# Windowed attention and a gated MLP: transposed probabilities spread into the band matrix by DMA, and the first entry's x split straight from PSUM

## The chip, the cores and the metric

One Trainium2 chip, one core. The metric is the device time of one launch in microseconds: the median of several runs for the kernel before, and the same for the changed one. Engines are called PE (TensorE), DVE (VectorE), ACT (ScalarE), POOL (GpSimd) and SP (SyncE, which issues the DMAs).

## What is computed

Attention over 8 batch entries, 8 heads, 576 positions of 64, with two masks, and then a gated MLP over all 4608 rows:

```python
scores = scale * q @ k.T                       # scale = 1/8
rel = pos[:, None] - pos[None, :]
mask_plain = (rel >= 0) & (rel < 32)                       # heads 0 to 3
mask_dil = (rel >= 0) & (rel < 128) & (rel % 4 == 0)       # heads 4 to 7
attn = softmax(where(mask, scores, -1e9)); attn_out = attn @ v
x = attn_out.transpose(0, 2, 1, 3).reshape(4608, 512)
h = x @ w_in                                   # 512 x 2048
g = h * sigmoid(1.702 * h)
out = g @ w_out                                # 2048 x 512
```

The weights come as float64.

## The kernel before

The host reorders the positions of the dilated heads by residue mod 4, so that each head has a band of 32 keys. The work has two kinds.

*Attention units.* A unit is one batch entry `b` and one pair of heads `c` (0 to 3), 32 in all, numbered i = 4b + c. `load_qk` and `load_v` fetch its inputs. `scores` makes blocks of 32 queries by 64 keys in PSUM (`sp`), `exponents` masks them (DVE, `pr` and the row minimum `mx`) and exponentiates (ACT, row sum `sm`); DVE normalises (`sm`, `pr`) and transposes the 32x32 blocks into `ct`. Then the transposed blocks are spread into `bt`, whose columns hold the probabilities as a band matrix with zeros elsewhere: eight copies per head or pair of heads, from one group of 32 partitions to another, on ACT or DVE. The two halves of `weigh` multiply `v` with `bt` on PE (24 matmuls, `av` in PSUM, "the product" below); ACT copies `av` to `xm` (512 of the entry's 576 positions) and to `xr` (the last 64, for a ninth group).

*MLP groups.* Eight groups of 512 positions (one per entry, `m0` to `m7`) and one of the 8 x 64 leftovers (`r`). `split_x` splits x into a float32r high part `xh` (ACT) and the remainder `xl` (DVE or POOL). For each of 16 slices f, `up` makes `hp` with 12 matmuls of 128x512 (4 blocks of x times 3: high by high, high by the weights' low part, low by high), ACT and DVE gate it, and `down` adds 12 more into four `acc` banks. A weight slice is decoded from float64 by `decode` (32 slices, n = 2f and 2f + 1): a load to a `cell`, three ACT passes and three or four DVE or POOL passes of 512 columns, giving `wih`, `wil`, `woh`, `wol`. All of this falls into the first group; entry 0's attention stands ahead of it, entry 1's beside it, and entry b + 1's attention runs beside group b from then on.

*Order.* Every step is an operation in `Plan` with a cost for each engine that may do it, an urgency, and keys that it reads and writes. `ordered` runs these through a list scheduler with those costs and emits each engine's instructions in that order; engines, and SP's queue of DMAs, work strictly in it. Waits come from the tile framework. DMAs count their completion on eight counters in turn, so each one waits for the one eight places earlier.

Units of entry 0 use `qk`, `v` and the buffer `second` in turn. There is one `pr`, `mx`, `sm`, `ct` and one `bt`.

Of the kernel before, what the change touches and what calls it, by code (L numbers as in the profile page):

```python
# [7 lines left out]
F32 = mybir.dt.float32  # L8
# [8 lines left out]
P = 128  # L17
# [14 lines left out]
class Plan:  # L32
# [27 lines left out]
    def ordered(self):  # L60
# [8 lines left out]
        port = [0.0]  # L69
# [11 lines left out]
        while any(open_):  # L81
# [10 lines left out]
            free[e] = when + (cost - 2.0 if e == DMA else cost)  # L92
# [12 lines left out]
def tile_windowed_attention_then_gated_mlp(  # L105
# [38 lines left out]
    xr = fixed([P, NC, B * LT], F32, "xr")  # L144
    pr = fixed([P, 2, QT, W], F32, "pr")
    mx = fixed([P, 2, QT], F32, "mx")
    sm = fixed([P, 2, QT], F32, "sm")
    ct = fixed([P, 2, QT, W], F32, "ct")
    bt = fixed([P, 2, QT, P + 32], F32, "bt")
# [19 lines left out]
    V.memset(sm, 1.0)  # L169
    V.memset(pr, 0.0)  # L170
    V.memset(bt, 0.0)
# [19 lines left out]
    def decode(n, urgency):  # L191
# [8 lines left out]
        else:  # L200
# [5 lines left out]
        taken = {8: ("qk1",), 9: ("qk1", "v1")}.get(n, ())  # L206
        low, top = (raw.bitcast(U32).rearrange("p (n t) -> p n t", t=2)[:, :, j] for j in range(2))
        value = word.bitcast(F32)

        add({DMA: 3.5}, urgency, lambda e: load(raw, src), (), (R, *taken))  # L210
# [8 lines left out]
            (R, R + "l"), (E,))  # L219
        add({ACT: 0.56}, urgency, lambda e: A.activation(hi, value, AF.Copy), (E,), (key,))  # L220
        add({DVE: -0.61, POOL: 1.35}, urgency, lambda e: pair(e, lo, value, f32(hi), ALU.subtract), (E,), (key,))

    def attention(b, c, urgency):
# [3 lines left out]
        z = i % 2 if b != 1 else 0  # L227

        spare = second.bitcast(F32).rearrange("p j n -> p (j n)")

        def load_qk(e):
            flat = spare[:, 0:2 * S] if z else temp([P, 2 * S], F32, "qk", f"qk_{i}")
            u["qk"] = flat.rearrange("p (a s) -> p a s", a=2)
            load(u["qk"], qk[i])

        def load_v(e):
            n = 2 * QT * D
            flat = spare[:, 2 * S:2 * S + n] if z else temp([P, n], F32, "v", f"v_{i}")
            u["v"] = flat.rearrange("p (a t d) -> p a t d", a=2, t=QT)
            load(u["v"], vp[i])  # L240


        late = [f"w{x}{f}" for x in "io" for f in range(NF - 3, NF)] if b >= FIRST else []
        add({DMA: 3.7}, urgency, load_qk, late if z else (), (f"qk{z}",))
        add({DMA: 3.0}, urgency, load_v, late if z else (), (f"v{z}",))

# [20 lines left out]
        def exponents(a, t):  # L267
            n = min(P, S - P * t)
            box, key = pr[0:n, a, t], f"{a}.{t}"
# [7 lines left out]
        def weights(hs):  # L277

            n, heads = hs.stop - hs.start, range(hs.start, hs.stop)
            boxes = [f"{a}.{t}" for a in heads for t in range(QT)]  # L280
# [7 lines left out]
            for a in heads:  # L288
                add({POOL: 0.69, DVE: -0.41}, urgency, lambda e, a=a: pair(
                    e, pr[:, a], pr[:, a], sm[:, a, :, None].broadcast_to([P, QT, W]), ALU.mult),  # L290
                    sums, [f"pr{a}.{t}" for t in range(QT)])
            turned = [f"ct{a}" for a in heads]
            for to in (0, 32):
                add({DVE: 0.07 + 0.165 * n}, urgency, lambda e, to=to: V.transpose(
                    out=ct[:, hs, :, to:to + 32], in_=pr[:, hs, :, 32 - to:64 - to]), probs, turned)
            for m in range(8):
                j, prev = m % 4, m // 4
                q = slice(32 * j, 32 * j + 32)
                if not prev:
                    dst, src = bt[q, hs, :, 32 * j:32 * j + 32], ct[q, hs, :, 0:32]  # L300
                elif j:
                    dst, src = bt[32 * j - 32:32 * j, hs, :, 32 * j:32 * j + 32], ct[q, hs, :, 32:64]
                else:
                    dst, src = bt[96:128, hs, 0:4, 128:160], ct[0:32, hs, 1:5, 32:64]
                add({ACT: 0.19 + 0.152 * n, DVE: -(0.19 + 0.07 * n)}, urgency,
                    lambda e, dst=dst, src=src: copy(e, dst, src), turned, [f"bt{a}{m}" for a in heads])

        for hs in (slice(0, 1), slice(1, 2)) if b < FIRST else (slice(0, 2),):
            weights(hs)

        def weigh(hf):
# [4 lines left out]
            def product(e):  # L316
                u["av", hf] = av = bank([P, 288], place, f"av_{i}_{hf}")
                for m, (t, lo, hi, col) in enumerate(parts):
                    for a in range(2):

                        T.matmul(av[D * a:D * a + D, col:col + hi - lo], u["v"][:, a, t], bt[:, a, t, lo:hi],  # L321
# [3 lines left out]
                (f"v{z}", *(f"bt{a}{m}" for a in range(2) for m in range(8))), (place, "product"))  # L325
            left = slice(LT * b, LT * b + LT)
            pieces = []
# [184 lines left out]
```

## Time and profile before

| | us |
|---|---|
| median of 3 runs | 925.05 (923.9 to 926.47) |
| profiled execution, its own time | 924.66 |
| its span, first to last instruction | 922.7 |
| PE busy | 892.7 (97%) |
| DVE, ACT, POOL busy | 494.7 (54%), 407.2 (44%), 30.1 (3%) |
| mean granted clock of PE | 0.985 |
| DMA, share of 16 engines | 18.5% in the one queue of SP |

The profile gives for each engine the time that its instructions cover. Matmuls are pipelined and overlap in the record, so a PE busy share near 100% is not yet PE at its peak rate; how many matmuls start in a stretch tells that. Idle time of an engine is listed with what released it.

### The profile page before, as it was taken

Reading aid. Unit: us, or ns where it says so; the run is one execution under the profiler, and the core shown is the slowest. Engines: PE = TensorE matmul, PEld = TensorE weight load, DVE = VectorE, ACT = ScalarE, POOL = GpSimd, SP = SyncE. Lnnn points to the kernel's source line nnn. Section 1 sums busy time; section 2 is a strip of 40 time slices with the busy share of each in tenths; the row PEclk is TensorE's granted clock in tenths of the full one; section 3 lists DMA queues with packets and bytes.
Section 4 is the critical chain, followed back from the end, with each engine's and each line's share of the span. In section 5 each row is a group of like instructions: output and inputs, shape, how many; then the busy total and the mean of one; then the engine's idle time right before and its main releaser. Section 6 shows DMA issues by size and latency. Waiting matters only on the chain.

```text
span 922.7 us, 17219 instructions
## 1 busy us (share of the span) xinstructions
PE 892.7 (97%) x6656; PEld 726.1 (79%) x6656; DVE 494.7 (54%) x1576; ACT 407.2 (44%) x1257; POOL 30.1 (3%) x32
## 2 busy tenths in 40 slices
PE   5699998999999999999999999999999999999997
PEld 4477786888888888888888888888888888888885
DVE  8899997655456337543654356534553433343332
ACT  7989878653366117621653156513641221121111
POOL 0011210000000000000000000000000000000000
PEclk9589999999999999999999999999999999999999
DMA  7365534211032003200221013100200010001002
GB/s 278 106 232 180 169 101 140 80 47 51 21 101 72 15 1 113 81 15 1 87 67 55 1 50 105 55 1 16 72 2 0 1 46 1 1 0 46 1 1 46
DMA packets 22674, 56.68 MB, mean 61 GB/s; under 512 B 6208, under 2 KB 6208, under 8 KB 22592
## 3 DMA queue, kind: packets, MB, share of 16 engines
q1 hardware_dynamic: 22592, 55.58, 18.5%
q8 instruction: 52, 0.85, 0.4%
q14 instruction: 30, 0.25, 0.1%
HBM read 46.14 MB, written 9.44 MB: 60 GB/s over the span
## 4 chain that ended last, share of the span: by engine, by line
PE 87%; ACT 5%; DVE 5%; DMA 1%; issue 1%; POOL 0%; DVEq 0%; SPq 0%; ACTq 0%
PE hp_m L369 36%; PE acc_m L406 12%; PE acc_m L407 12%; PE acc_m L410 12%; PE hp_r L369 5%; PE av L321 4%; PE sp L260 3%; PE acc_r L410 2%; PE acc_r L406 2%; PE acc_r L407 2%; ACT pr L273 1%; ACT bt L175 1%; DVE words L216 1%; DVE words L218 1%; DVE bt L177 1%
## 5 line engine op out<-in xcount | busy, mean ns | idle before, releaser
L376 ACT ACTIVATE g_m<-hp_m 128x512 f32<-128x512 f32 x128 | 76.1, 595 | 323.6 <-PE hp_m L369 323.3
L369 PE MATMUL hp_m<-xh,wih 128*128 128x512 f32 x512 | 206.4, 403 | 11.3 <-ACT xh L175 7.2
L379 DVE SCALAR_TENSOR_TENSOR g_m<-g_m,hp_m 128x512 f32<-128x512 f32 x128 | 87.8, 686 | 232.0 <-ACT g_m L376 230.9
L369 PE MATMUL hp_m<-xh,wil 128*128 128x512 f32 x512 | 201.8, 394 | 0.6 <-POOL wil L182 0.6
L369 PE MATMUL hp_m<-xl,wih 128*128 128x512 f32 x512 | 201.8, 394 | 0.0
L406 PE MATMUL acc_m<-gh_m,woh 128*128 128x512 f32 x512 | 201.2, 393 | 0.1
L407 PE MATMUL acc_m<-gh_m,wol 128*128 128x512 f32 x512 | 199.4, 389 | 0.0
L410 PE MATMUL acc_m<-gl_m,woh 128*128 128x512 f32 x512 | 142.3, 391 | 0.0
L369 PEld LDWEIGHTS hp_m<-xh,wih 128*128 128x128 f32 x512 | 97.0, 190 | 36.0 <-ACT xh L175 8.1
L273 ACT ACTIVATE pr<-pr,mx 128x64 f32<-128x64 f32 (+1 forms) x320 | 106.8, 336 | 32.5 <-DVE mx L270 32.4
L369 PEld LDWEIGHTS hp_m<-xl,wih 128*128 128x128 f32 x512 | 97.2, 190 | 22.1 <-DVE xl L182 1.6
L369 PEld LDWEIGHTS hp_m<-xh,wil 128*128 128x128 f32 x512 | 97.2, 190 | 20.1 <-POOL wil L182 1.1
L406 PEld LDWEIGHTS acc_m<-gh_m,woh 128*128 128x128 f32 x512 | 96.1, 188 | 21.1 <-ACT gh_m L175 0.3
L410 PEld LDWEIGHTS acc_m<-gl_m,woh 128*128 128x128 f32 x512 | 95.9, 188 | 20.5 <-POOL gl_m L182 0.2
L407 PEld LDWEIGHTS acc_m<-gh_m,wol 128*128 128x128 f32 x512 | 96.1, 188 | 19.6
L182 DVE TENSOR_TENSOR gl_m<-g_m,gh_m 128x512 fp32r<-128x512 f32 x126 | 90.0, 714 | 15.9 <-ACT gh_m L175 7.2
L270 DVE CUSTOM_DVE_ANT_0 pr<-sp,mask 128x64 f32<-128x64 f32 (+1 forms) x320 | 49.4, 213 | 49.0 <-PE sp L260 48.8
L175 ACT ACTIVATE bt<-ct 32x320 f32<-32x320 f32 (+3 forms) x171 | 70.3, 411 | 3.1
L273 ACT ACTIVATION_READ_ACCUMULATOR pr<-pr,mx 128x1 f32 (+1 forms) x320 | 60.3, 188 | 0.0
L177 DVE CAST gh_m<-g_m 128x512 fp32r<-128x512 f32 x107 | 45.5, 425 | 8.0
L175 ACT ACTIVATE xm<-av 128x224 f32<-128x224 f32 (+1 forms) x64 | 32.0, 505 | 30.6 <-PE av L321 30.6
L177 DVE COPY bt<-ct 32x320 f32<-32x320 f32 (+3 forms) x149 | 44.0, 295 | 2.6
(75 smaller groups left out, 782.6 us busy)
## 6 DMA issues: line engine op xcount, KB each, us to landing
qk<-qk_dram SPq DMA_DIRECT2D x18, 576.0 KB, 4.6
out_dram<-ost_m SPq DMA_DIRECT2D x32, 256.0 KB, 2.1
second<-qk_dram SPq DMA_DIRECT2D x14, 576.0 KB, 4.2
v<-vp_dram SPq DMA_DIRECT2D x18, 320.0 KB, 3.0
cell<-wi_dram SPq DMA_DIRECT2D x11, 512.0 KB, 3.7
cell<-wo_dram SPq DMA_DIRECT2D x11, 512.0 KB, 3.9
second<-vp_dram SPq DMA_DIRECT2D x14, 320.0 KB, 3.1
second<-wi_dram SPq DMA_DIRECT2D x5, 512.0 KB, 4.7
```

What stands on the lines that cost most here:

```text
L175: A.activation(dst, src, AF.Copy, scale=scale)
L177: V.tensor_copy(out=dst, in_=src)
L182: (V if e == DVE else G).tensor_tensor(out=dst, in0=a, in1=b, op=op)
L270: add({DVE: 0.15}, urgency, lambda e: V.tensor_tensor_reduce(out=box, in0=u["sp", a][0:n, t], in1=mask[0:n, t if dil or t == 0 else QT - 1 ...
L273: add({ACT: 0.33}, urgency, lambda e: A.activation(box, box, AF.Exp, bias=mx[0:n, a, t:t + 1], scale=-1.0, accum_out=sm[0:n, a, t:t + 1]), ...
L321: T.matmul(av[D * a:D * a + D, col:col + hi - lo], u["v"][:, a, t], bt[:, a, t, lo:hi], start=m == 0, stop=m == 2, skip_group_check=True)
L369: T.matmul(hps[f], st[:, f, c], mv[:, c], start=c == 0 and k == 0, stop=c == NC - 1 and k == 2)
L376: A.activation(self.g32, hps[f], AF.Tanh, scale=0.851)
L379: V.scalar_tensor_tensor(out=self.g32, in0=self.g32, scalar=1.0, in1=hps[f], op0=ALU.add, op1=ALU.mult)
L406: T.matmul(self.acc[j], woh[:, f, cols], gh, start=f == 0, stop=False)
L407: T.matmul(self.acc[j], wol[:, f, cols], gh, start=False, stop=False)
L410: T.matmul(self.acc[j], woh[:, f, P * j:P * j + P], self.g[f][1], start=False, stop=f == NF - 1)
```

## The change

Three things, and a new order that follows from them.

1. The eight copies from `ct` to `bt` become eight DMAs on SP's queue for a whole unit (`spread`), each 32 partitions by 320 elements (one has two pieces of 128). `ct` gets the two transposed halves as separate contiguous pieces and `bt` is laid out by column group, so that a partition's data is one run. `pr`, `mx`, `sm`, `ct` exist twice (by i mod 2). Entry 0 also has two `bt`; the second lies in the part of `wol` that the last four slices fill later, and POOL clears it.
2. For entry 0, `xh` and `xl` are made from `av` in PSUM directly, without `xm` and without `split_x`.
3. All inputs of entry 0 are loaded at once, units 2 and 3 into `xm` and `xr`, which are not otherwise used yet; weight slices 1 and 2 are ordered after the first spread.

The scheduler's model of a DMA changes: the queue is held 0.43 us, and the transfer takes 2.0 us and its size over a shared bus.

The diff, its core:

```diff
-            free[e] = when + (cost - 2.0 if e == DMA else cost)
+            free[e] = when + (0.43 if e == DMA else cost)
+            if e == DMA:
+                bus[0] = max(bus[0], when + 2.0) + cost / 360.0
+                cost = bus[0] - when
...
-    ct = fixed([P, 2, QT, W], F32, "ct")
-    bt = fixed([P, 2, QT, P + 32], F32, "bt")
+    cts = [fixed([P, 2, 2, QT, 32], F32, f"ct{j}") for j in range(2)]
+    late_bt = wol[:, NF - 4:].bitcast(F32).rearrange("p f n -> p (f n)")[:, 0:10 * QT * 32]
+    bts = [fixed([P, 5, 2, QT, 32], F32, "bt"), late_bt.rearrange("p (j a t n) -> p j a t n", j=5, a=2, t=QT)]
...
+    G.memset(late_bt, 0.0)
...
+    spare = [second.bitcast(F32).rearrange("p j n -> p (j n)"), xm.rearrange("p c n -> p (c n)"),
+             xr[:, 1:].rearrange("p b c n -> p (b c n)")]
...
-        z = i % 2 if b != 1 else 0
+        z = i if b == 0 else 0 if b == 1 else i % 2
+        y = i % 2 if b == 0 else 0
+        pr, mx, sm, ct, bt = prs[i % 2], mxs[i % 2], sms[i % 2], cts[i % 2], bts[y]
...
-            for to in (0, 32):
-                add({DVE: 0.07 + 0.165 * n}, urgency, lambda e, to=to: V.transpose(
-                    out=ct[:, hs, :, to:to + 32], in_=pr[:, hs, :, 32 - to:64 - to]), probs, turned)
+            for half in (0, 1):
+                add({DVE: 0.07 + 0.165 * n}, urgency, lambda e, half=half: V.transpose(
+                    out=ct[:, half, hs], in_=pr[:, hs, :, 32 - 32 * half:64 - 32 * half]),
+                    probs, [f"ct{i % 2}{half}{a}" for a in heads])
+
+        def spread():
             for m in range(8):
                 j, prev = m % 4, m // 4
                 q = slice(32 * j, 32 * j + 32)
                 if not prev:
-                    dst, src = bt[q, hs, :, 32 * j:32 * j + 32], ct[q, hs, :, 0:32]
+                    dst, src = bt[q, j], ct[q, 0]
                 elif j:
-                    dst, src = bt[32 * j - 32:32 * j, hs, :, 32 * j:32 * j + 32], ct[q, hs, :, 32:64]
+                    dst, src = bt[32 * j - 32:32 * j, j], ct[q, 1]
                 else:
-                    dst, src = bt[96:128, hs, 0:4, 128:160], ct[0:32, hs, 1:5, 32:64]
-                add({ACT: 0.19 + 0.152 * n, DVE: -(0.19 + 0.07 * n)}, urgency,
-                    lambda e, dst=dst, src=src: copy(e, dst, src), turned, [f"bt{a}{m}" for a in heads])
+                    dst, src = bt[96:128, 4, :, 0:4], ct[0:32, 1, :, 1:5]
+                add({DMA: 82}, urgency, lambda e, dst=dst, src=src: load(dst, src),
+                    [f"ct{i % 2}{prev}{a}" for a in (0, 1)], (f"bt{y}{m}", f"spread{i}.{m}"))
...
-                        T.matmul(av[D * a:D * a + D, col:col + hi - lo], u["v"][:, a, t], bt[:, a, t, lo:hi],
+                        T.matmul(av[D * a:D * a + D, col:col + hi - lo], u["v"][:, a, t],
+                                 bt[:, lo // 32:hi // 32, a, t],
...
+            if b == 0:
+                n = x_cols.stop - x_cols.start if not dil else 2 * P
+                add({ACT: 0.07 + n * 0.00083}, urgency, lambda e: copy(e, x_place(xh), x_of(u["av", hf])),
+                    (place,), (f"xh{c}.{hf}",))
+                add({DVE: 0.07 + n / 960}, urgency, lambda e: pair(
+                    e, x_place(xl), x_of(u["av", hf]), f32(x_place(xh)), ALU.subtract),
+                    (place, f"xh{c}.{hf}"), (f"xl{c}.{hf}",))
...
-    for n in range(2):
-        decode(n, 9.0 + n)
     for c in range(NC):
-        attention(0, c, 6.0 * c)
+        attention(0, c, c)
+        if c in (1, 2):
+            decode(c - 1, c + 0.5)
```

PE's order at the start, from the third unit's scores on. Before (L260 scores, L321 the product, L369 `up`; `64x160 x4` are four matmuls with 64 output rows and 160 columns):

```order
L260 MATMUL sp_0_246<-qk_194 32x32 x2
L260 MATMUL sp_0_246<-qk_194 32x64 x17
L260 MATMUL sp_1_279<-qk_194 32x32 x2
L260 MATMUL sp_1_279<-qk_194 32x64 x17
L321 MATMUL av_1_313<-bt,v_112 64x128 x2
L321 MATMUL av_1_313<-bt,v_112 64x160 x2
L321 MATMUL av_1_313<-bt,v_112 64x64 x2
L321 MATMUL av_0_331<-bt,v_112 64x160 x4
L321 MATMUL av_0_331<-bt,v_112 64x32 x2
L260 MATMUL sp_0_347<-second 32x32 x2
L260 MATMUL sp_0_347<-second 32x64 x17
L260 MATMUL sp_1_385<-second 32x32 x2
```

And now (L275 scores, L340 the product):

```order
L275 MATMUL sp_0_322<-xr 32x32 x2
L275 MATMUL sp_0_322<-xr 32x64 x17
L275 MATMUL sp_1_356<-xr 32x32 x2
L275 MATMUL sp_1_356<-xr 32x64 x17
L340 MATMUL av_1_390<-bt,v_119 64x128 x2
L340 MATMUL av_1_390<-bt,v_119 64x160 x2
L340 MATMUL av_1_390<-bt,v_119 64x64 x2
L340 MATMUL av_0_412<-bt,v_119 64x160 x4
L340 MATMUL av_0_412<-bt,v_119 64x32 x2
L340 MATMUL av_1_435<-wol,second 64x128 x2
L340 MATMUL av_1_435<-wol,second 64x160 x2
L340 MATMUL av_1_435<-wol,second 64x64 x2
```

The scores of all four units now stand ahead of the first product, and the first two products follow each other. By the fourth product 18 matmuls of `up` stood ahead before, and 12 now.

SP's order at the start, before, from its fifth DMA (L210 weight slices, L234 and L240 inputs):

```order
L210 DMA cell_104<-wi_dram 128x512
L210 DMA cell_105<-wo_dram 128x512
L234 DMA qk_194<-qk_dram 128x1152
L210 DMA cell_106<-wi_dram 128x512
L234 DMA second<-qk_dram 128x1152
L234 DMA qk_322<-qk_dram 128x1152
L210 DMA cell_104<-wo_dram 128x512
L240 DMA v_371<-vp_dram 128x640
```

And now, from its ninth DMA, with the waits (L323 is the spread; DMAHW0 to DMAHW7 are the eight completion counters):

```order
L254 DMA xr<-vp_dram 128x640 [waits DMAHW0_49]
L220 DMA second<-wi_dram 128x512 [waits DMAHW2_49,DMAHW1_49,PE_49]
L323 DMA bt<-ct_80 32x320 [waits DVE_49]
L323 DMA bt<-ct_80 32x320 [waits DMAHW3_49]
L323 DMA bt<-ct_80 32x320 [waits DMAHW4_49]
L323 DMA bt<-ct_80 32x320 [waits DMAHW5_49]
L323 DMA bt<-ct_80 32x2x128 [waits DMAHW6_49,DVE_49]
L323 DMA bt<-ct_80 32x320 [waits DMAHW7_49]
L323 DMA bt<-ct_80 32x320 [waits DMAHW0_49]
L323 DMA bt<-ct_80 32x320 [waits DMAHW1_49]
```

Ten loads stand ahead of the first spread; its eighth DMA shares a counter with the tenth load. The second unit's spread follows, and then three weight slices.

PE's order in the steady part, before, at the product of unit 9 (entry 2, c = 1):

```order
L369 MATMUL hp_m_4_2058<-xh,wih 128x512
L369 MATMUL hp_m_4_2058<-xh,wil 128x512
L369 MATMUL hp_m_4_2058<-xl,wih 128x512
L321 MATMUL av_1_2067<-bt,second 64x128 x2
L321 MATMUL av_1_2067<-bt,second 64x160 x2
L321 MATMUL av_1_2067<-bt,second 64x64 x2
L321 MATMUL av_0_2074<-bt,second 64x160 x4
L321 MATMUL av_0_2074<-bt,second 64x32 x2
L260 MATMUL sp_0_2083<-qk_1819 32x32 x2
```

And now:

```order
L407 MATMUL hp_m_5_2033<-xh,wih 128x512
L407 MATMUL hp_m_5_2033<-xh,wil 128x512
L407 MATMUL hp_m_5_2033<-xl,wih 128x512
L340 MATMUL av_1_2037<-bt,second 64x128 x2
L340 MATMUL av_1_2037<-bt,second 64x160 x2
L340 MATMUL av_1_2037<-bt,second 64x64 x2
L340 MATMUL av_0_2044<-bt,second 64x160 x4
L340 MATMUL av_0_2044<-bt,second 64x32 x2
L407 MATMUL hp_m_5_2033<-xh,wih 128x512
```

The product has moved from the middle of `hp` 4 to that of `hp` 5: between a unit's scores and its product stand 42 to 45 matmuls of 128x512 before and 52 to 62 now.

97 lines of the change are left out of this document (54 added, 43 removed).

## The prediction

> **What bounds the kernel now.** I read the stretches first (busy time of each engine per window, granted clock, DMA share).
>
> ```profile
> 20.00:30.00 10.00, 6.05 (x29) 4.26 (x30) 9.61 (x44) 9.80 (x41) 0.82 (x1) 0.53 0.68 226
> 30.00:40.00 10.00, 6.91 (x34) 4.52 (x33) 8.26 (x46) 9.78 (x37) 1.28 (x1) 0.62 0.21 71
> ...
> 100.00:150.00 50.00, 47.81 (x306) 37.34 (x305) 48.83 (x139) 43.35 (x119) 8.27 (x8) 1.00 0.37 118
> ...
> 200.00:300.00 100.00, 99.88 (x882) 81.66 (x881) 56.01 (x204) 49.14 (x169) 1.28 (x1) 1.00 0.18 58
> ```
>
> The columns are PE, PEld, DVE, ACT, POOL, clock, DMA share, GB/s. There are three regimes. From 200 us PE is full: 99.88 of 100 us. From 20 to 40 us ACT and DVE are full (ACT 9.80 of 10 us) and PE is not, at a clock of 0.53 to 0.62. From 53 to about 165 us, where the weights are still being decoded, DVE is nearly full (48.83 of 50) and PE loses a little. Then PE's own waits and its timeline, for the places:
>
> ```profile
> PE hp_m L369 <- ACT xh L175: 7.2, 3, 2.6
> PE sp L260 <- DMA qk<-qk_dram: 4.7, 1, 4.7
> PE hp_m L369 <- DVE g_m L379: 3.1, 2, 1.5
> ```
>
> ```profile
> 14.72 2.69 PE L321 MATMUL av<-bt,v 128*64 128x128 f32 x24
> ...
> 34.77 2.67 PE L321 MATMUL av<-bt,v 128*64 128x128 f32 x24
> ...
> 43.16 2.63 PE L321 MATMUL av<-bt,second 128*64 128x128 f32 x22 [0.72 <-DVE bt L177]
> 46.12 0.80 PE L369 MATMUL hp_m<-xh,wih 128*128 128x512 f32 x1 [0.33 <-ACT wih L220]
> ...
> 51.55 0.39 PE L369 MATMUL hp_m<-xh,wih 128*128 128x512 f32 x1
> ...
> 53.12 0.76 PE L260 MATMUL sp<-qk 64*32 64x32 f32 x38
> ```
>
> The named waits are short; what is lost at the start is mostly PE idling or at half clock behind a chain of ACT and DVE work: the fourth value product of batch entry 0 runs only at 43.16, and the 36 matmuls of the first three `hp` tiles are over at 53.12. Matmuls of 0.80 us become 0.39 at about 51.5, five microseconds after steady work began at 46.12. In the full regime the rate is
>
> ```profile
> 826.65 2.72 PE hp_r L369 x12
> ...
> 165.45 1.46 PE L321 MATMUL av<-bt,v 128*64 128x128 f32 x24
> ```
>
> 0.227 us each (2.72/12). The first row is from the chain that ended last, the second from PE's timeline: the first product of entry 2, the 430th matmul's place in program order, after which nothing is lost. So only the first 165 us can be won; behind them stands the same PE work whichever kernel runs, unless new waits appear there.
>
> **The change, part by part.** (1) The copies `bt<-ct` go from ACT and DVE. Busy time of the instructions that touch `bt` (PE, PEld, DVE, ACT):
>
> ```profile
> 0.00:60.00 60.00, 12.01 (x96) 10.49 (x96) 9.94 (x36) 9.52 (x29) 0.77 0.58 196
> 60.00:200.00 140.00, 11.48 (x168) 9.95 (x168) 12.43 (x39) 17.84 (x49) 1.00 0.41 135
> 200.00:922.70 722.70, 30.63 (x504) 28.45 (x504) 23.02 (x75) 42.91 (x93) 1.00 0.11 36
> ```
>
> That is 9.5 us of ACT and 9.9 of DVE (one memset, which stays, among it) before 60 us, and 17.8 and 12.4 between 60 and 200. After 200 us the 66 us lie under a full PE and are worth nothing.
>
> (2) In their place 8 DMAs for each of 32 units go on SP's queue, 256 in all. What one costs, the trace of before bounds only by other transfers: the spacing of issues, and time from issue to landing.
>
> ```profile
> 1.19 0.42 SPq L240 DMA_DIRECT2D v<-vp_dram  x1
> 1.65 0.43 SPq L234 DMA_DIRECT2D second<-qk_dram  x1
> ```
>
> ```profile
> out_dram<-ost_m SPq DMA_DIRECT2D x28, 256.0 KB, 2.1
> qk<-qk_dram SPq DMA_DIRECT2D x9, 576.0 KB, 4.6
> ...
> v<-vp_dram SPq DMA_DIRECT2D x9, 320.0 KB, 2.9
> ```
>
> Issues stand 0.46 us apart. A 40 KB spread between on-chip buffers lies nearest to the 256 KB store (2.1 us), below it if anything; 4.6 us (qk) is the far end, and zero the near one. I take 2.1: eight cost 7 x 0.46 + 2.1 = 5.3 us from `ct` to a usable `bt`, of which ACT and DVE pay nothing. A page of the Trainium skill speaks against the change: "SBUF — State Buffer", The DMA setup-cost knee, has each DMA pay a fixed 2 us or so and advises 128 partitions and one large transfer. By its figures (an estimate: 2 us + 41 KB at 218 GB/s for 32 partitions) one spread lands after 2.2 us, and the sum would not move by more than 0.1 us a unit.
>
> (3) At the start the queue matters. Six loads were issued by 3.7 us, and landed so (issue to landing):
>
> ```profile
> qk<-qk_dram SPq DMA_DIRECT2D x1, 576.0 KB, 4.0
> second<-qk_dram SPq DMA_DIRECT2D x1, 576.0 KB, 6.3
> cell<-wo_dram SPq DMA_DIRECT2D x1, 512.0 KB, 8.1
> ...
> second<-qk_dram SPq DMA_DIRECT2D x1, 576.0 KB, 5.9
> 9.95 0.33 SPq L234 DMA_DIRECT2D second<-qk_dram  x1
> ```
>
> A load waits for the bytes ahead of it: the ninth, issued at 9.95, landed at 15.85, with 4.6 MB through. In the changed kernel ten loads (4.7 MB) precede the first spread, so the tenth lands at about 16.1. And the rows of SP's order show that each DMA waits for the one eight places earlier; the eighth spread of unit 0 therefore waits for the tenth load.
>
> ```profile
> 9.59 1.25 DVE L177 COPY bt<-ct 32x160 f32<-32x160 f32 x5
> ...
> 12.25 0.34 DVE L294 STREAM_TRANSPOSE ct<-pr 128x160 f32<-128x160 f32 x1
> 6.34 0.35 ACT L273 ACTIVATE pr<-pr,mx 128x64 f32<-128x64 f32 x1 [4.32 <-DVE mx L270]
> ...
> 6.68 0.33 ACT L273 ACTIVATE pr<-pr,mx 128x64 f32<-128x64 f32 x1
> L175 ACT ACTIVATE xh<-xm 128x512 fp32r<-128x512 f32 x4 | 2.5, 620 | 0.0
> cell<-wi_dram SPq DMA_DIRECT2D x11, 512.0 KB, 3.7
> ```
>
> Unit 0's `ct` was complete at 12.6 with five copies (1.25 us) ahead of it on DVE, so now at 11.4. But its last spread is issued at 16.1 and lands at 18.2: the first product moves from 14.72 to 18.3, 3.6 us later. Then ACT, no longer interrupted by copies, runs the 40 exponentials 0.34 us apart from 6.34 on, with decode passes of 512 columns (0.62 us, as the `xh` row) between. Unit 1: `ct` at about 15.7, SP free at 16.6, spread landed at 22.3. Unit 2: exponentials over at 6.3 + 30 x 0.34 + 4 x 0.62 = 19.0, with half a microsecond of waiting 19.5; sums, product and transposes on DVE and POOL, `ct` near 22.2; three weight loads were issued at 20.2 to 21.2 and its last spreads wait for them (3.7 us for the first and more behind it, about 26.5): product at 28.7, where before it ran at 34.77. Unit 3: ten more exponentials, three decode passes and four of x, 19.5 + 3.4 + 3 x 0.62 + 4 x 0.6 = 27.1, `ct` near 28.8 by DVE's 1.7 us behind them, eight issues, landing at 34.5: product from 34.6 to 37.3, where before it ended at 45.8. The split of x from PSUM drops one ACT pass of 512 columns per c (the `xh` row, 0.62) and makes two subtractions where there was one on DVE; worth 0.5 us for the last c, inside the rounding. Of the 36 matmuls, 24 then stand behind the fourth product (18 before): 6 at half clock until about 40 us (five microseconds after steady work), 18 at 0.227: done at 44.0. **Gain to this point 53.1 - 44.0 = 9.1 us.** Bounds: 14 (no queueing, clock up at once) and 2 (the spread landing at 4.6 us in all four units, 10 us, less what the next unit's exponentials cover).
>
> (4) The decode stretch. From 53.12 to 165.45 PE does 393 matmuls (89.1 us) and
>
> ```profile
> 53.12:165.45 112.33, 6.74 (x380) 5.47 (x380) 1.00 0.47 155
> ...
> 53.12:165.45 112.33, 7.10 (x96) 5.90 (x97) 1.00 0.47 155
> ```
>
> 6.7 us of scores and 7.1 of products (first column after the length), 102.9 of 112.3: 9.4 us are lost, to gates that come late (the 3.1 above) and many small ones, with DVE nearly full. DVE and ACT lose about 12 and 18 us of work there. I take 4 us back. Bounds: 9.4 (all), and 3 us worse: weight loads now queue on SP behind spreads that wait for DVE's transposes, and a late decode is a late `hp`.
>
> (5) The steady part. The order puts the product of a unit 52 to 62 matmuls behind its scores (42 to 45 before).
>
> ```profile
> 275.62 1.00 PE L260 MATMUL sp<-second 64*32 64x32 f32 x76
> 286.98 1.46 PE L321 MATMUL av<-bt,second 128*64 128x128 f32 x24
> 282.28 0.90 DVE L294 STREAM_TRANSPOSE ct<-pr 128x320 f32<-128x320 f32 x2
> 283.63 2.39 ACT L175 ACTIVATE bt<-ct 32x320 f32<-32x320 f32 x5
> ```
>
> `ct` was ready at 283.2, the copies at 286.0, the product started at 286.98: 0.96 us of slack. With 54 matmuls for 45 it starts 2.0 us later, 5.8 us behind `ct`; 5.3 are needed. Cost nothing, by half a microsecond a unit. The cover is those matmuls; if it is gone, PE stands still for the difference in each of 24 units.
>
> The other parts cost nothing at the place where they stand: a POOL memset of 1600 columns runs while DVE waits for the first scores; smaller `pr` memsets lie before the first load lands; a second `pr`, `ct`, `bt` takes memory only. Later scores of units 2 and 3 need no buffer of unit 0 any more, which is in the walk.
>
> Sum on the profiled execution: 924.66 (span 922.7 and 1.96 around it) - 9.1 - 4.0 = 911.6; the median of the runs stands 0.4 higher, so 912.0.
>
> **Rivals.** *Steady stalls* (slower). If a spread lands later than about 2.6 us after issue, PE, which takes its work in order, waits in each of 24 units. At 2.9 us, the `v` row, 0.3 x 24 = 7 us come back; at 4.6, 2.0 x 24 = 48 us (947). It decides at 3.2 us, where 0.55 x 24 = 13 eats the gain. For it: the spread lies behind the next qk load in the same queue. Against it: that load is issued right behind the scores, 7 us earlier, and the nearest row, the store, has 2.1. Chance 0.10; time about 935.
> *The start gains little* (920 to 926): the queue holds the spreads back in every unit and the weight loads behind them in turn, so the gain of (3) is 2 and (4) is nothing or a loss. For it: 3.6 us are already lost on unit 0. Against it: from 20 us on the stretches show the DMA at a share of 0.21 to 0.68. Chance 0.12; about 922.
> *The decode stretch recovers fully* and the start is at its better bound: 924.7 - 11 - 9 = 905 or below; chance 0.06.
> *Spreads one after another.* If the fixed cost were paid eight times in series, a unit would need 8 x 2.1 = 17 us, 11 more than the order leaves: 24 x 11 = 264 us. The landings above (4.7, 8.0 and 11.3 us for the first, third and sixth of six loads, with 0.6, 1.5 and 2.9 MB through) go by bytes and overlap, so 0.01. The same page of the Trainium skill, in the rule that a DMA-bound transfer should be one DMA and not several, would make the kernel slower in this way; the trace does not agree for loads in flight together.
>
> **How the numbers follow.** My forecast, 905 to 920 about 912: 0.70. With the other cases and 0.01 for what I don't see, faster by over 0.3% (2.8 us; about what a measurement of this kernel can tell) gets 0.70 + 0.06 + 0.07 of the second rival, within 0.3% gets 0.05 of it, slower 0.10 + 0.01 + 0.01. The range reaches from the better bound, 902, to the second rival's worse end, 925; outside are the steady stalls.
>
> **What would show it.** First product near 18 us, fourth near 35, the first `acc` matmuls near 44; spreads landing near 2 us; DVE under 90% busy between 50 and 150; PE still 99.8% from 200 us on with no wait of `av` on a DMA. Wrong if a spread takes over 2.6 us, if `av <- DMA bt` stands among PE's waits in the steady part, or if decodes (`wih`, `woh`) become the wait of `hp` behind late weight loads.

## The result and the profile after

The changed kernel takes 935.08 us (median of 4 runs, 933.65 to 937.55), the kernel before 925.76 in the same rounds: a ratio of 1.0106, 95% interval 1.0078 to 1.0134. It is 9 us slower; 13 us faster had been forecast, and the range ended at 925. The profiled execution of the changed kernel is its longest, 937.55 us with a span of 935.8, so differences between the two traces (13.1 us of span) come out some 4 us larger than between the medians.

The stretches that the prediction read, now of the changed kernel (length, then PE, PEld, DVE, ACT, POOL busy, clock, DMA share, GB/s):

```profile
20.00:30.00 10.00, 6.53 (x50) 5.39 (x46) 6.99 (x42) 7.23 (x34) 0.72 (x1) 1.00 0.61 207
30.00:40.00 10.00, 6.35 (x33) 4.47 (x33) 8.36 (x18) 6.02 (x13) 0.00 (x0) 0.53 0.53 166
100.00:150.00 50.00, 49.06 (x332) 38.87 (x331) 39.36 (x89) 32.45 (x70) 7.22 (x6) 1.00 0.40 129
200.00:300.00 100.00, 98.90 (x870) 79.52 (x869) 44.96 (x164) 36.67 (x139) 2.25 (x2) 1.00 0.23 73
```

ACT and DVE did get their time back: ACT 7.23 of 10 us for 9.80 at the start, DVE 39.36 of 50 for 48.83 in the decode stretch. But PE is no fuller at the start, and from 200 us on it is 98.90 instead of 99.88. PE's waits name a new releaser (us in total, times, longest):

```profile
PE av L340 <- DMA bt<-ct: 10.5, 8, 2.9
PE sp L275 <- DMA qk<-qk_dram: 4.8, 2, 4.6
```

The products and the first `acc` matmul at the start, on PE's timeline (start, us, ...):

```profile
19.28 2.67 PE L340 MATMUL av<-bt,v 128*64 128x128 f32 x24 [2.90 <-DMA bt<-ct]
...
24.10 2.67 PE L340 MATMUL av<-wol,second 128*64 128x128 f32 x24 [2.16 <-DVE sm L302]
...
32.35 2.67 PE L340 MATMUL av<-bt,xm 128*64 128x128 f32 x24 [1.91 <-DMA bt<-ct]
...
39.98 1.87 PE L340 MATMUL av<-wol,xr 128*64 128x128 f32 x24
...
50.14 0.50 PE L445 MATMUL acc_m<-gh_m,woh 128*128 128x512 f32 x1
```

To see where the time goes I counted the 3456 matmuls of 128x512 (9 groups x 16 slices x 24) along PE's timeline and noted when the 37th, 769th and 3456th start. Their order among the attention work shifts a little between kernels, so the stretch from 769th to 3456th, 2688 matmuls with the steady attention beside them, is the clean one: in the runs below that keep the order of before it takes 660.5, 669.2 or 673.8 us, to within 0.1, and nothing between.

| start of matmul | 37th | 769th | 3456th | 769th to 3456th |
|---|---|---|---|---|
| before | 54.0 | 255.6 | 916.0 | 660.5 |
| changed | 50.1 | 253.5 | 929.9 | 676.3 |

So 3.9 us are won by the 37th matmul, 2.1 are left at the 769th, and 15.8 are lost in the part where the prediction had put zero. The first two columns scatter between executions: in before and three runs below with its order and its matmul length (256 and 5120 bytes, all tiles by 128) the 37th starts at 53.2 to 54.0 us and the 769th at 255.6 to 258.1, so 2 us at the 769th are within what single traces differ by. The last column is 660.5 in all four.

The loss of 15.8 us has two causes, as the experiments show. One is late spreads. The other is in no step of the prediction: even in the last group `r`, with no attention, no spread and no wait beside it, the matmuls are longer. Rows of PE by form, before (busy, mean ns):

```profile
L406 PE MATMUL acc_r<-gh_r,woh 128*128 128x512 f32 x64 | 24.9, 389 | 0.0
L407 PE MATMUL acc_r<-gh_r,wol 128*128 128x512 f32 x64 | 24.9, 389 | 0.0
...
L410 PE MATMUL acc_r<-gl_r,woh 128*128 128x512 f32 x64 | 17.6, 389 | 0.0
```

and changed:

```profile
L445 PE MATMUL acc_r<-gh_r,woh 128*128 128x512 f32 x64 | 25.4, 397 | 0.0
L446 PE MATMUL acc_r<-gh_r,wol 128*128 128x512 f32 x64 | 25.0, 391 | 0.0
...
L449 PE MATMUL acc_r<-gl_r,woh 128*128 128x512 f32 x64 | 18.0, 395 | 0.0
```

The three kinds of `hp_r` have 390 ns, for 389 before.

These instructions are the same in both kernels. Only the addresses differ: the second `pr`, `mx`, `sm` and `ct` take 2560 + 64 + 64 + 2560 bytes a partition, and everything allocated after `bt` (mask, second, words, g, ost, qk, v, gh, gl) has moved by these 5248 bytes; the weights and x have not.

### The profile page after: what moved, and what is told of

It is laid out like the page before. It is cut to its first block, busy times and chain, and to the rows that moved or that the text cites. A ratio compares the mean times of both kernels' runs of the same rounds, so it can differ in the third digit from the quotient of the medians.

```text
span 935.8 us, 17232 instructions
## 1 busy us (share of the span) xinstructions
PE 901.7 (96%) x6656; PEld 725.4 (78%) x6656; DVE 452.8 (48%) x1425; ACT 338.9 (36%) x1087; POOL 34.6 (4%) x36
## 4 chain that ended last, share of the span: by engine, by line
PE 82%; DVE 5%; ACT 4%; DMA 4%; SPq 2%; issue 1%; DVEq 0%; ACTq 0%
PE hp_m L407 33%; PE acc_m L445 11%; PE acc_m L449 11%; PE acc_m L446 11%; PE hp_r L407 5%; PE av L340 4%; PE sp L275 2%; SPq L323 2%; ACT pr L288 2%; PE acc_r L445 2%; PE acc_r L449 2%; PE acc_r L446 2%; DMA bt<-ct 1%; DMA second<-wi_dram 1%; DMA cell<-wo_dram 1%
## 5 line engine op out<-in xcount | busy, mean ns | idle before, releaser
L445 PE MATMUL acc_m<-gh_m,woh 128*128 128x512 f32 x512 | 205.9, 402 | 0.0
L407 PE MATMUL hp_m<-xl,wih 128*128 128x512 f32 x512 | 201.5, 394 | 0.1
L449 PE MATMUL acc_m<-gl_m,woh 128*128 128x512 f32 x512 | 144.7, 395 | 0.0
L407 PEld LDWEIGHTS hp_m<-xl,wih 128*128 128x128 f32 x512 | 96.7, 189 | 22.3 <-DVE xl L190 1.2
L183 ACT ACTIVATE xm<-av 128x256 f32<-128x256 f32 (+2 forms) x56 | 28.0, 505 | 64.1 <-PE av L340 63.9
L185 DVE CAST gh_m<-g_m 128x512 fp32r<-128x512 f32 x96 | 41.0, 427 | 8.9
L418 DVE SCALAR_TENSOR_TENSOR g_r<-g_r,hp_r 128x512 f32<-128x512 f32 x16 | 11.0, 688 | 55.8 <-ACT g_r L415 55.8
L340 PEld LDWEIGHTS av<-bt,v 128*64 128x64 f32 x408 | 25.2, 144 | 15.3 <-issue 10.9
```

The source lines that it names most:

```text
L183: A.activation(dst, src, AF.Copy, scale=scale)
L185: V.tensor_copy(out=dst, in_=src)
L407: T.matmul(hps[f], st[:, f, c], mv[:, c], start=c == 0 and k == 0, stop=c == NC - 1 and k == 2)
L418: V.scalar_tensor_tensor(out=self.g32, in0=self.g32, scalar=1.0, in1=hps[f], op0=ALU.add, op1=ALU.mult)
L445: T.matmul(self.acc[j], woh[:, f, cols], gh, start=f == 0, stop=False)
L449: T.matmul(self.acc[j], woh[:, f, P * j:P * j + P], self.g[f][1], start=False, stop=f == NF - 1)
```

## The experiments

Each was timed in five rounds against the kernel before on the same chip; ratios are to those runs (medians of before 925.3 to 926.1).

### Does placement cost time? The kernel before, with unused tiles

**5248 bytes behind `bt`.** `+ pad = fixed([P, 1312], F32, "pad")`, nothing else.

> The kernel before with one unused tile of 5248 bytes a partition behind `bt`, so that every tile allocated after it (mask, second, words, g, gh, gl and so on) lies at the address that it has in the changed kernel; no instruction is different. Theory of placement (the 128x512 matmuls of the MLP start 0.8% further apart in the changed kernel, 0.236 for 0.228 us on the first product with gh, because gh and gl lie elsewhere): the same pitches as in the changed kernel, about 6 to 7 us more than before, near 932, faster or slower alike in every stretch. Rival (the pitch belongs to the execution or to the chip, not to the addresses): 925 to 926, pitch 0.2277.

Measured 934.35, ratio 1.0094 (1.0082 to 1.0106); 769th to 3456th 669.2 us, 8.7 more than before. An unused tile alone costs as much as the whole change.

**128 and 5120 bytes** (their sum is 5248): `[P, 32]` and `[P, 1280]` in the same place.

> The kernel before with an unused tile of only 128 bytes a partition behind `bt`: gh starts at 213248 instead of 213120, so that its address modulo 512 is 256 as in the run with 5248 bytes, while it lies practically where it lay. Theory of phase (what counts is where gh, gl and the other moved tiles start modulo 512 bytes: the weights and x stand at 128): slow, as with 5248 bytes, 933 to 935, gh,woh to gh,wol 0.236 us apart. Rival (what counts is the region of the memory): as before, 925 to 926, 0.2277 us.

> The kernel before with an unused tile of 5120 bytes a partition behind `bt`: gh starts at 218240, 128 bytes from where the run with 5248 bytes has it, at the phase modulo 512 of the kernel before (128). Theory of phase: as before, 925 to 926, 0.2277 us. Rival (region): slow, 933 to 935, 0.236 us.

128 bytes: 935.11, 1.0103 (1.0089 to 1.0117), stretch 669.2. 5120 bytes: 925.79, 0.9997 (0.9987 to 1.0007), stretch 660.5. The phase counts, not the region.

**256 bytes; 128 bytes ahead of all tiles; 128 bytes ahead of gh and gl alone.** `[P, 64]` behind `bt`; `[P, 32]` ahead of `wih`; and

```diff
+                if f == 0 and self is main[0]:
+                    temp([P, 32], F32, "pad", "pad")
                 gh = temp([P, GT], F32R, f"gh{f % 2}", f"gh_{self.name}_{f}")
```

> The kernel before with an unused tile of 256 bytes a partition behind `bt`: gh starts at 384 modulo 512, at 128 modulo 256 as before. If the period is 256 bytes: as before, 925 to 926. If it is 512 or more: slow, 930 to 936.

> The kernel before with an unused tile of 128 bytes a partition ahead of all tiles: weights, x, gh, gl and the rest all move by 128 bytes together. Theory of relative phase (gh and gl must stand as the weights and x do): as before, 925 to 926. Theory of absolute phase (an operand at 0 modulo 256 is slow): slow in hp and acc alike, 3456 matmuls by at least 9 ns on most, 933 to 960.

> The kernel before with an unused tile of 128 bytes a partition between v and gh, so that gh and gl alone move by 128 bytes; mask, second, words, g, ost, qk and v stay. Theory (the phase of the matmul's moving operand decides): slow by the full amount, 933 to 935. Rival (the phase of a tile that ACT, DVE or the DMA write decides, such as g or second): 925 to 926.

256 bytes: 926.06, 1.0005 (0.9996 to 1.0015), stretch 660.5. All tiles moved by 128: 924.53, 0.9993 (0.9983 to 1.0002), 660.5. gh and gl alone: 936.82, 1.0116 (1.0101 to 1.013), 669.3. So the period is 256 bytes or a part of it, the phase is relative to something in place ahead of `bt`, and gh and gl, the moving operands of `down`, are the tiles that matter. PE by form in the run with gh and gl alone moved has the changed kernel's numbers:

```profile
L408 PE MATMUL acc_r<-gh_r,woh 128*128 128x512 f32 x64 | 25.4, 397 | 0.0
L409 PE MATMUL acc_r<-gh_r,wol 128*128 128x512 f32 x64 | 25.0, 391 | 0.0
...
L412 PE MATMUL acc_r<-gl_r,woh 128*128 128x512 f32 x64 | 18.0, 395 | 0.0
```

Over the six kinds (hp three times +1 ns, then +8, +2, +6 ns over 389) that is 3.2 ns a matmul; times 2688 it makes 8.5 us, against 8.7 to 8.8 measured in the stretch.

**The weights alone by 128 bytes; gh and gl by 64.**

```diff
+    pad = fixed([P, 32], F32, "pad")
     wih = fixed([P, NF, NC, P], F32R, "wih")
...
+    pad2 = fixed([P, 32], F32, "pad2")
     xh = fixed([P, NC, GT], F32R, "xh")
```

> The kernel before with an unused tile of 128 bytes a partition ahead of the four weight tiles and another behind them: the weights alone start at 0 modulo 256, and x, xh, xl, gh, gl and the rest, moved by 256 bytes, stay at 128. Theory (moving operand and weights of a matmul must stand alike modulo 256): now the matmuls of hp and acc are all out of phase, twice as many as with gh and gl alone, so twice the cost, 940 to 950, and 0.236 us also between hp's matmuls. Rival (gh must stand like x or another tile that the moved weights leave alone): 925 to 926.

> The kernel before with gh and gl alone moved by 64 bytes: they start at 192 modulo 256, the weights at 128. If any offset other than a multiple of 256 bytes is out of phase: 930 to 937. If only an offset of 128 is (a period with two halves): 925 to 926.

Weights alone: 941.59, 1.0168 (1.0155 to 1.0182), stretch 673.8, 13.4 more than before: 1.5 times what gh and gl alone cost (8.7), where twice had been expected. Now `hp` is slow as well, which had 390 ns when gh moved:

```profile
L371 PE MATMUL hp_r<-xh,wil 128*128 128x512 f32 x64 | 25.3, 395 | 0.0
...
L408 PE MATMUL acc_r<-gh_r,woh 128*128 128x512 f32 x64 | 25.2, 394 | 0.0
```

gh and gl by 64 bytes: 935.7, 1.0109 (1.0096 to 1.0122), stretch 669.2. So the phase that costs time is that between the moving operands and the weights, and 64 bytes are enough. One thing does not fit the simplest form of this: with 64 bytes, two of the three kinds of `hp` matmuls, both of whose operands stand where they stood, are long too (396, 389 and 394 ns):

```profile
L369 PE MATMUL hp_r<-xh,wih 128*128 128x512 f32 x64 | 25.4, 396 | 0.0
```

so it isn't only an affair of one matmul's own two operands. That a matmul streams while the next one's weights are read would allow it (in the trace of before PE is busy 892.7 us and its weight loads 726.1 us of a span of 922.7, so they overlap); this is argued, not shown, and the mechanism stays open.

### The changed kernel, put back in phase

**Second copies behind the temporary tiles** (a second pool for `pr`, `mx`, `sm`, `ct` number 1), which restores the addresses of before; and, with one line, **384 bytes behind `bt`**, which makes the shift 5632 = 22 x 256:

```diff
+    pad = fixed([P, 96], F32, "pad")
     mask = fixed([P, QT, W], BF16, "mask")
```

> The changed kernel with the second copies of pr, mx, sm and ct allocated behind the temporary tiles, so that mask, second, words, g, gh and gl are back at the addresses of the kernel before; order of instructions untouched. Theory of placement: pitch back to 0.2277 us, 6 to 7 us less than the changed kernel, near 928. Rival (pitch of the execution or chip): 935, no change. A third theory, that spreads written into SBUF beside the matmuls slow them, gives 935 as well, with the pitch of the changed kernel wherever spreads run and that of before in the last group.

> The changed kernel with one edit, an unused tile of 384 bytes a partition behind `bt`, so that its tiles stand 5632 bytes (22 x 256) behind those of the kernel before instead of 5248 (20.5 x 256). Theory of phase: the same as with the second copies moved behind the temporary tiles, 927 to 930, acc_r matmuls 389 ns long; what is left over the kernel before, 3 to 4 us, is the late spreads. Rival (the other placement gained through the place of pr, mx, sm and ct): 934 to 936.

929.38, ratio 1.0041 (1.0029 to 1.0053), and 929.88, 1.0042 (1.0026 to 1.0058). All acc_r rows are back at 389 ns in both. Against the changed kernel's 1.0106, placement is 0.0064, 5.9 us; in the traces' steady stretch it is 9.0 (667.3 for 676.3). The two differ in part because the traced execution of the changed kernel was its slowest. What is left, 0.4%, is the change itself: 667.3 is 6.8 us over 660.5.

### Late spreads

**The planner told that a DMA holds SP's queue for 0.7 us**, alone and with the tiles in phase:

```diff
-            free[e] = when + (0.43 if e == DMA else cost)
+            free[e] = when + (0.7 if e == DMA else cost)
```

> The changed kernel with the planner told that a DMA holds SP's queue 0.7 us instead of 0.43, all else alike: it puts a unit's product 60 to 72 matmuls behind its scores. Theory (the eight issues of a spread take 5.1 to 5.8 us on SP, with 1.9 to land, against about 5.8 us that the order left): the waits of `av` on the DMA go from 250 us on, about 8 us less than the changed kernel, near 927; the start stays as it is. Rival (the spreads disturb PE while they run, whenever they land): within 2 us of the changed kernel.

> The changed kernel with two edits together: the second copies of pr, mx, sm and ct behind the temporary tiles (placement of the kernel before for the rest), and SP's queue held 0.7 us a DMA by the planner. Theory (placement costs 6 to 9 us, late spreads what is left of the steady part, and the start keeps its gain): no wait of `av` from 250 us on, pitch 0.2277, and the 3456 matmuls done 4 to 9 us before the changed kernel with placement alone: 921 to 925. Rival (moving the products further back costs at the start and in the decode stretch what the waits cost now): 928 to 930, no better than placement alone.

Alone: 933.97, 1.009 (1.0076 to 1.0105). The expected 927 was missed: the stretch fell to 669.7 (660.5 + 8.7 of phase + 0.5), but "the start stays as it is" did not hold. The new order holds for the start too; the 37th matmul starts at 55.0 instead of 50.1 and the 769th at 256.9 instead of 253.5. At the start PE now waits for ACT's copies of the product (`xr` 3.8 us, `xh` 2.7, for 0 and 1.2); why those are late stays open. In phase: 923.0, 0.9971 (0.9959 to 0.9984), stretch 660.8, as full as before. Waits of `av` between 250 and 800 us, 384-byte version and then in phase with the hold:

```profile
PE av L341 <- DMA bt<-ct: 3.3, 6, 1.3
PE av L341 <- issue: 1.8, 4, 0.7
```

```profile
PE av L341 <- DMA bt<-ct: 0.3, 1, 0.3
```

So the spreads cost PE nothing in this stretch as soon as the product stands far enough behind: the waits were lateness, not a disturbance of PE by the transfers. The waits for the spread and for "issue" make 5.1 of the 6.8 us of the 384-byte version; the profile names no wait for most of the rest.

**Spread by DMA for entry 0 alone**, copies from entry 1 on, out of phase and in phase:

```diff
+                if b == 0:
+                    add({DMA: 82}, urgency, lambda e, dst=dst, src=src: load(dst, src), *keys)
+                else:
+                    add({ACT: 0.494, DVE: -0.33}, urgency, lambda e, dst=dst, src=src: copy(e, dst, src), *keys)
```

> The changed kernel with the spread by DMA kept for batch entry 0 only; from entry 1 on the copies go to ACT and DVE as in the kernel before. Theory (late spreads make PE wait at `av`, and each long wait is followed by a lower clock): the waits of `av` on the DMA and the clock drops near 74 and 466 us are gone, 8 to 13 us less than the changed kernel, 922 to 927. Rival (the loss in the steady part is the longer pitch alone, not the waits): 1 or 2 us less, 933 to 934.

> The changed kernel with two edits together: spreads by DMA for batch entry 0 alone (copies on ACT and DVE from entry 1 on), and the placement of the kernel before. Theory: pitch 0.2277, no wait of `av` on a DMA from 60 us on; 6 to 9 us less than the hybrid with the changed placement, 926 to 929, since the hybrid's start was only 1.5 us ahead of the kernel before at the 36th matmul and behind it at the 120th. Rival (the hybrid loses for another reason than placement): 933 to 935.

Out of phase: 934.88, 1.0097 (1.0082 to 1.0113); near the rival's 933 to 934, and the expected 922 to 927 was missed. I had counted the phase as 6 to 7 us in the steady part and the waits as 8 to 13; the stretch is 671.6: the waits are gone (0.2 us listed from 250 us on), the 8.7 of phase is still in, and 2.4 us have no wait to their name. In phase: 928.27, 1.0029 (1.0017 to 1.004), as expected, but its stretch is 664.4, 3.9 over before, with no spread in it: there 2.9 us are short waits of `av`, in part for copies. A late operand costs PE time whichever way it comes.

### SP's queue at the start

**Units 0 and 2 by copies again, units 1 and 3 by DMA**, on top of the version in phase with the hold:

```diff
+                if b == 0 and y == 0:
+                    add({ACT: 0.494, DVE: -0.33}, urgency, lambda e, dst=dst, src=src: copy(e, dst, src), *keys)
+                else:
+                    add({DMA: 82}, urgency, lambda e, dst=dst, src=src: load(dst, src), *keys)
```

> The changed kernel with the placement and the queue hold of the fast version, and in batch entry 0 the spread by DMA only for units 1 and 3; units 0 and 2, whose target is the first `bt`, go back to copies on ACT and DVE. Theory (at the start SP's queue is the bound: 11 to 38 us in one row, four spreads of 5.1 to 6.5 us with the weight loads between them): SP is free 12 us earlier in all, the first product is back near 15, the 36th MLP matmul is done near 46 to 48 instead of 54.6, and the time is 916 to 921. Rival (ACT and DVE are the bound at the start, as the prediction had it, and copies cost there what SP saves): 923 to 926.

Measured 920.25, 0.994 (0.9923 to 0.9958), the fastest of all. Against the version it is built on (0.9971) that is 0.0031, 2.9 us. In the traces the 37th matmul starts at 50.9 instead of 55.0 (46 to 48 was expected, so the gain there is smaller), the 769th at 249.1 instead of 253.6, 4.5 us earlier, of which some may be scatter; the stretch is 660.5. Its products on PE's timeline, and its spreads on SP's:

```profile
14.21 2.67 PE L344 MATMUL av<-bt,v 128*64 128x128 f32 x24
25.79 2.67 PE L344 MATMUL av<-wol,second 128*64 128x128 f32 x24 [4.92 <-DMA wol<-ct]
29.02 1.44 PE L344 MATMUL av<-bt,xm 128*64 128x128 f32 x12 [0.57 <-DVE xl L191]
...
40.22 1.46 PE L344 MATMUL av<-wol,xr 128*64 128x128 f32 x24 [0.87 <-DMA wol<-ct]
```

```profile
18.95 5.19 SPq L328 DMA_DIRECT2D wol<-ct  x8
...
33.75 5.05 SPq L328 DMA_DIRECT2D wol<-ct  x8
```

The products of the two units with copies run earlier than in the version it is built on (14.21 for 19.75, 29.02 for 30.45). Of the other two, the second is little earlier (25.79 for 26.33) and the fourth later (40.22 for 36.88), and both wait for a DMA, 4.92 and 0.87 us.

## Why the prediction was wrong

On the profiled executions 13.1 us less had been forecast and 12.9 more were measured. Most of these 26 us stand at two terms of the prediction. "A second `pr`, `ct`, `bt` takes memory only" put at nothing what costs 8.7 us behind the 769th matmul, through the place of other tiles; and "5.3 are needed" of the 5.8 us that the order leaves, in (5), was mis-sized: a plain spread needs 6.0, the slowest took 8.6, and late spreads cost 6.8 us. The start (3) gave 3.9 of its 9.1 us and the decode stretch (4) none of its 4 that could be told from scatter. That the time is the 935 of the rival "steady stalls" is chance, since that rival had the stalls alone and kept the gain before them.

**(1) The copies.** Right: ACT's busy time fell from 407.2 to 338.9 us and DVE's from 494.7 to 452.8.

**(2) The price of a spread.** This is the first step that failed, and one number in it. The landing was right in the median, 1.9 us for the 2.1 taken; the long ones are at the start (median 3.7 in the first 45 us), where (3) had them wait behind loads:

```profile
DMA to landing us min/median/max: 1.8/1.9/6.1
```

The spacing of issues was not: 0.46 was taken from loads. With nothing in their way, SP took 5.05 us for a spread's eight, 0.63 each. SP's timeline of the changed kernel, the four spreads of entry 0 and two of the steady part:

```profile
11.08 6.26 SPq L323 DMA_DIRECT2D bt<-ct  x8
17.45 5.07 SPq L323 DMA_DIRECT2D wol<-ct  x8
...
24.20 6.49 SPq L323 DMA_DIRECT2D bt<-ct  x8
...
31.88 5.75 SPq L323 DMA_DIRECT2D wol<-ct  x8
...
273.04 5.06 SPq L323 DMA_DIRECT2D bt<-ct  x8
...
288.90 5.76 SPq L323 DMA_DIRECT2D bt<-ct  x8
```

The longer rows hold more than issues. In the first and third SP also waited for the load eight places earlier, which shares the counter (SP's waits from 11 to 38 us):

```profile
SPq L323 <- DMA cell<-wo_dram: 1.5, 1, 1.5
...
SPq L323 <- DMA second<-wi_dram: 0.9, 1, 0.9
...
SPq L323 <- DMA xr<-vp_dram: 0.4, 1, 0.4
```

In the fourth, and in that of 288.90, one of the eight issues took 1.3 us; the longest of the run took 2.2. Why, the traces don't show.

The trace of before had issues on both sides of the one taken. Its stores, from which the landing came, held SP for 0.33 us each, and those of the last group, which have eight pieces a partition, for 0.65 (least, median and most, in ns):

```profile
L428 SPq DMA_DIRECT2D out_dram<-ost_m x32: 332/333/703, 150.6 to 832.8; - x32
```

```profile
L428 SPq DMA_DIRECT2D out_dram<-ost_r x4: 617/651/1127, 915.1 to 917.3; - x4
```

No row said which of them a spread would be like. With the second as the far end a spread is 7 x 0.65 + 2.1 = 6.7 us, more than the 5.8 that the order leaves: a bound on the issues, as there was one on the landing, would have put a loss into (5).

**(3) The start.** 3.9 us instead of 9.1, and 3.0 and 2.9 in the two versions in phase: near the rival "the start gains little", which had 2 us and 0.12, and by its mechanism, the queue. The first product (18.3 forecast, 19.28) and the second (after 22.3, 24.10) are near; the third is 3.6 us late (28.7, 32.35) and the fourth 5.4 (34.6, 39.98). SP's rows above say why: from 11.08 to 37.6 us its queue is taken almost without a gap, 23.6 us of it by spreads; without the 2.8 of waits for loads, which the prediction had in its walk, these are 20.8, where 4 x 3.7 = 14.7 had been counted. The weight loads between the spreads come late in turn, and ACT waits for those:

```profile
26.18 0.66 ACT L221 ACTIVATE words<-cell 128x512 f32<-128x512 f32 x1 [2.63 <-DMA cell<-wo_dram]
...
34.41 0.66 ACT L222 ACTIVATE second<-second 128x512 uint32<-128x512 uint32 x1 [2.27 <-DMA second<-wo_dram]
```

The last four exponentials of unit 3 stand behind the first of these on ACT, and its `ct` was complete at 31.8 for the 28.8 forecast. The bound at the start went from ACT and DVE to SP's queue: taking two units' spreads off the queue gave 2.9 us.

**(4) The decode stretch.** 4 us were to come back between the 37th and the 769th matmul. The changed kernel takes 203.4 us there (its 732 matmuls at 3.2 ns more make 2.3 of it), the two versions in phase 202.4 and 201.5; before and the three runs with its order and matmul length take 201.6 to 204.6. So little or nothing came back, and one trace each can't say how much. What the lower bound named is seen, though not with its price: in the 384-byte version scores at 68.68 wait 2.18 us for `qk`, in the changed kernel a product at 73.57 waits 1.76 us for its spread, and the clock falls to 0.50 afterwards in both. Against that, DVE with 79% busy in the stretch from 100 us did let PE run fuller (49.06 of 50 for 47.81).

**(5) The steady part.** "Cost nothing, by half a microsecond a unit" failed through the spacing. A plain spread, as that of 273.04 above, lands its last DMA 6.3 us after its first issue, which goes out 0.37 us before `ct` is complete (273.04, 273.41 and 279.38): 6.0 us are needed, for 5.3 forecast and 5.8 left. So such a unit just comes in time or a little late, and any delay on SP becomes a wait of PE. A unit of the changed kernel with such a delay, DVE's and then PE's timeline:

```profile
288.37 0.90 DVE L308 STREAM_TRANSPOSE ct<-pr 128x320 f32<-128x320 f32 x2
```

```profile
296.25 1.46 PE L340 MATMUL av<-bt,second 128*64 128x128 f32 x24 [0.85 <-issue]
```

`ct` is complete at 289.27 and the product starts 7.0 us later; the spread is the one with an issue of 1.3 us. In one unit of each later entry two stores of the result stand between the spread's DMAs, and in that of the longest wait, 1.92 us, an issue of 2.2 us comes on top (SP's timeline):

```profile
457.01 1.15 SPq L323 DMA_DIRECT2D bt<-ct  x2
458.25 1.01 SPq L467 DMA_DIRECT2D out_dram<-ost_m  x2
459.31 5.41 SPq L323 DMA_DIRECT2D bt<-ct  x6
```

In sum 6.8 us (the 384-byte version's stretch over 660.5). That is the mechanism of the rival "steady stalls", which had 0.10; but it named the wrong half of the spread, the landing, whose median stayed at 1.9 us from 200 us on (most 4.1, the only one of 168 over its 3.2). Its 947 us for a landing of 4.6 don't follow from its own sum either: 912 + 48 is 960.

**What no step had.** The prediction said of the second `pr`, `ct` and `bt` that they "take memory only". They moved gh and gl by 20.5 x 256 bytes, which costs 8.7 us in the steady part. No row of the trace of before could have shown this, but that allocation moves other tiles was in the diff, and no chance was kept for it beyond the 0.01. Without it and with the loss of (5) the changed kernel is at 1.0042; with neither, 0.9971; with SP relieved at the start, 0.994. Of the signs named, the median landing and DVE's relief came; the first product was near (19.28), the fourth product, the first `acc` and PE's 99.8% were not.

## What to carry to other kernels

Price a DMA by its issue as well as its landing, with a range for both (here 0.33 to 0.65 us for an issue in the trace of before), and multiply by all that stand in the queue: eight small DMAs at 0.63 us are a 5 us block for everything behind them. Take the issue from single records: a merged row of DMAs also holds the time in which the queue waited (a row of four stores in 2.37 us of the trace of before has issues of 0.33 to 0.34 us, with waits for ACT between). After a change in tile sizes, compare the durations of instructions that did not change; if matmuls are longer with no wait beside them, look at addresses, and try keeping moving operands and weights at the same start modulo 256 bytes, as the fast runs here have them (a padding tile of some bytes is the test). Try a change again after taking out such a side effect, since the change itself may be sound: here the same spreads went from 1.0106 to 0.9971 with another placement and one number in the planner.

## What the runs showed of the hardware

*Placement and matmul length.* Differences of 0, 256, 5120 and 5632 bytes from the placement of before ran at the full rate (the 2688 matmuls with their attention in 660.5 us, but for waits), 64, 128 and 5248 for gh and gl at 669.2, 128 for the weights at 673.8: 0, 3.2 and 5.0 ns a matmul of 227. The Trainium skill's page "SBUF — State Buffer", Operand start alignment, lets an operand start at any multiple of its element size and says that this is about legality and that nothing was timed; these runs add a time, though not the cause.

*The clock after a short wait.* A wait of 1.92 us in the middle of full work was followed by matmuls at half clock in the changed kernel (PE's timeline; then two stretches of 3.4 us, with PE's busy time behind the length and the granted clock third from the end):

```profile
466.13 1.46 PE L340 MATMUL av<-bt,second 128*64 128x128 f32 x24 [1.92 <-DMA bt<-ct]
467.51 0.80 PE L407 MATMUL hp_m<-xh,wih 128*128 128x512 f32 x1
```

```profile
464.11:467.52 3.41, 1.49 (x26) 1.38 (x25) 0.00 (x0) 0.47 (x2) 0.00 (x0) 1.00 0.14 36
467.52:470.93 3.41, 3.41 (x83) 2.47 (x81) 0.47 (x7) 0.61 (x2) 0.00 (x0) 0.50 0.32 96
```

A longer one, of 2.68 us before 69.36 in the version with the second copies behind the temporary tiles, was not:

```profile
64.70:68.12 3.42, 1.98 (x9) 1.31 (x7) 2.84 (x9) 3.42 (x13) 1.00 (x1) 1.00 0.73 273
68.12:71.53 3.41, 2.17 (x81) 1.92 (x82) 2.47 (x5) 1.50 (x7) 0.00 (x0) 1.00 0.29 88
71.53:74.94 3.41, 3.41 (x17) 2.56 (x17) 2.59 (x5) 3.41 (x12) 0.00 (x0) 1.00 0.45 108
```

The stretches are laid on steps of 3.41 us, counted from a change of the granted clock in the same trace: it is at 0.50 from 74.99 to 78.40 and from 467.52 to 470.93 us in the changed kernel, one step each, and in the other trace it rises at 44.22. The wait of 1.92 us lay within one step, that of 2.68 us across two, 1.4 and 1.2 us in each. Idle time within one step does not decide alone either: in the run with units 0 and 2 by copies PE was idle as long within one, and the next stayed at 1.00:

```profile
65.78:69.19 3.41, 1.48 (x7) 0.90 (x5) 3.41 (x9) 3.41 (x16) 0.00 (x0) 1.00 0.64 208
69.19:72.60 3.41, 3.33 (x86) 2.81 (x86) 3.41 (x8) 2.63 (x11) 0.00 (x0) 1.00 0.54 152
```

The Trainium skill, "TensorE: Matmul & The Clock Gate", Part 1, lets the clock fall after an idle window of about 3.4 us that runs free of the kernel. That a wait's length alone does not decide, and that the clock changes in steps of 3.41 us, agrees with a free-running window; that 1.92 us idle in one can be enough is shorter than the page has it. What decides between these cases stays open.
